# Issuing the K and V cache loads of an attention decode kernel from GpSimd instead of SyncE

## The chip, the cores and the metric

The kernel runs on one core of one Trainium2 chip. The metric is the device time of one execution in microseconds (us). A core has five engines that run their own instruction streams and meet at semaphores: TensorE (PE; its weight loads are shown apart as PEld), VectorE (DVE), ScalarE (ACT), GpSimd (POOL) and SyncE (SP). Sixteen DMA engines move data between the chip's memory (HBM) and the on-chip buffer of 128 partitions. A DMA is *issued* by an instruction in the stream of SP, ACT or POOL; the sixteen engines then work through its packets. SP's and ACT's DMAs have hardware descriptors, POOL's have descriptors that GpSimd's own software writes.

## What is computed

One new token goes through a gated mix of two blocks: attention over a long cache, and a small gated feed-forward network. With 32 heads, 65,536 cached positions and a head width of 128, the two caches hold 1,073.7 MB in bf16, and every byte is read once. The rest is small.

```python
q = (x @ wq).reshape(B, Sq, H, Dh)                       # 1 x 512 by 512 x 4096
scores = einsum("bhqd,bhkd->bhqk", q, k_cache) * Dh**-0.5  # H=32, Sk=65536, Dh=128
p = softmax(scores, axis=-1)
o = einsum("bhqk,bhkd->bhqd", p, v_cache)
a = o.reshape(B, Sq, H * Dh) @ wo                        # 4096 x 512
b = (silu(x @ w_gate) * (x @ w_up)) @ w_down             # 512 x 1792
g = sigmoid((x * gate_w).sum(-1))
return g * a + (1 - g) * b
```

## The kernel before

**Storage and halves.** One tile, `mem`, takes all loads. K and V of a head are each cut into two halves, z = 0 and z = 1. A half is 128 partitions of 256 positions of 128 bf16 values, so 65,536 bytes a partition in one run, 8.39 MB in all. There is one buffer for each of the four kinds of half, and they overlap in part: K's halves lie at `KA` and `KZ`, V's at `VA` and `VZ`. A load into a buffer can only start when what it overwrites has been read.

**The work on one head.** VectorE transposes K in sixteen chunks, eight for each half (`L329` for head 0, `L397` for z = 0 and `L404` for z = 1 of the others), into the double buffer `kt`. TensorE turns each chunk into scores (`L454`, 32 matmuls). `ktdone` counts transposed chunks, `qkdone` scored ones. When all scores of a head stand in `psS`, VectorE takes their maximum by partition (`L343`, counted by `s_mx`), GpSimd takes the maximum over the partitions (`L273`, `s_ar`), ScalarE scales it (`L298`), takes the exponentials with their sums (`L300`, `expdone`) and fetches the next head's query (`L303`, counted by `s_qc`), and GpSimd adds the sums over the partitions (`L275`, `s_L`). VectorE then shuffles the probabilities in two lots of 16 small copies (`L338`), one in the middle of the next head's first half of K and one after it. TensorE multiplies with V (`L501`, `pvdone`) one head later than the scores: V's half z of head h-1 is used right after the scores of half z of head h. Its 64 matmuls for each half stand in two parts, 40 and then 24, and each part raises `pvdone` by one, from a start value of 4.

**Loads.** SP issues nearly all of them, in one queue and in a fixed order. First come four weights (`L203`: wq, w_gate, w_up, w_down), then head 0's first K half in two pieces (`L217`), and then the loop's loads, all through one helper whose issue is `L213`. The order within the loop for head h is K z=0 of head h, V z=0 of head h-1, K z=1 of head h, V z=1 of head h-1. In front of each stands a wait for the work that frees its buffer:

```python
sp.wait_ge(ktdone, 2 * NP * h - 3 if h > 1 else NP);  load("k", h, 0)
sp.wait_ge(pvdone, 4 * h - 1);                        load("v", h - 1, 0)   # h > 1
sp.wait_ge(ktdone, 2 * NP * h + NP // 2);             load("k", h, 1)
sp.wait_ge(pvdone, 4 * h + 1);                        load("v", h - 1, 1)
```

Here `NP` is 8. After the loop come `wo` (`L235`), the last head's V in eight pieces (`L242`) and two rows of `wo` (`L244`, `L245`). ACT issues the loads of x and of the gate's weights, and the store of the output.

**GpSimd before.** It makes a few constant tiles at the start (`L249` to `L269`, among them the masks at `L255`), and then does nothing but its two sums over the partitions for each of the 32 heads. Ahead of the first mask and ahead of the first sum stands an instruction that makes a different set of GpSimd's routines ready (`MODIFY_POOL_CONFIG` in the trace).

Of the kernel before, what the change touches and what calls it, by code (L numbers as in the profile page):

```python
# [5 lines left out]
P = 128  # L6
KB = 512
PR = 32
NG = PR // 4

ALU = mybir.AluOpType
ACT = mybir.ActivationFunctionType
# [8 lines left out]
def bass_gated_mix__mha_block_cached__swiglu_ffn__decode_kernel(  # L21
# [11 lines left out]
    out: bass.AP,  # L33
):
    _, H, S, Dh = A_k_cache.shape
    D = A_wq.shape[0]
    F = B_w_gate.shape[1]
# [3 lines left out]
    HR = R // 2  # L41
    NP = HR // PR
# [5 lines left out]
    KA, KZ, VA, VZ, V0 = 32, 0, 120, 96, 96  # L48
# [10 lines left out]
    tail = [(32, 0, 128), (0, 128, 128), (V0 + 24, 256, 128), (V0 + 64, 384, 64),  # L59
            (V0 + 80, 448, 32), (V0 + 56, 480, 16), (V0 + 60, 496, 12), (V0 + 63, 508, 4)]  # L60
    WOJ, WO31 = V0, V0 + 1

    with ExitStack() as ctx:
# [6 lines left out]
        def sem(name):  # L70
            return ctx.enter_context(nc.semaphore(name))
# [35 lines left out]
        def at(kb, n):  # L107
            return mem[:, kb * KB:kb * KB + n]
# [9 lines left out]
        d = {n: sem("d_" + n) for n in names}  # L118
        dt_ = [sem(f"d_t{i}") for i in range(len(tail))]
# [16 lines left out]
        s_q = sem("s_q")  # L136
# [7 lines left out]
        s_b = sem("s_b")  # L144
        s_dch = sem("s_dch")
        ktdone = sem("ktdone")
        qkdone = sem("qkdone")
        pvdone = sem("pvdone")
# [26 lines left out]
        w_dram = {  # L175
            "wq": A_wq.rearrange("(p c) n -> p (c n)", c=Dc),
            "wg": B_w_gate.rearrange("(p c) f -> p (c f)", c=Dc),
            "wu": B_w_up.rearrange("(p c) f -> p (c f)", c=Dc),
            "wd": B_w_down.rearrange("(p c) n -> p (c n)", c=FC),
            "wo": A_wo.rearrange("(p j) n -> p (j n)", p=P),  # L180
        }
        wj_dram = w_dram["wo"][:, 31 * D:32 * D]
        w31_dram = A_wo.rearrange("(h d) n -> h d n", d=Dh)[H - 1]
        WQ, WG, WU, WD, WO = V0, 0, 14, V0 + 64, 64
# [5 lines left out]
        w2_ap = at(WOJ, 2 * D).rearrange("p (e c n) -> p e c n", e=2, c=4)  # L190
        ktb = [kt[:, b, :].bitcast(BF16).rearrange("p (j r m e) -> p j r m e", j=2, r=NG, e=2) for b in range(2)]

        def place(kind, h, z):
            if kind == "k":
                return (KA, V0)[z] if h == 0 else (KA, KZ)[z]
            return (VA, VZ)[z]

        def kv_dram(cache, h):
            return cache[0, h].rearrange("(b p r) d -> b p (r d)", b=2, p=P)

        for n, kb in (("wq", WQ), ("wg", WG), ("wu", WU), ("wd", WD)):
            src = w_dram[n]
# [3 lines left out]
        ctx.callback(lambda: nc.scalar.wait_ge(s_out, 16))  # L206
        block = ctx.enter_context(nc.Block())

        @block.sync
        def _(sp):  # L210
            def load(kind, h, z):
                cache = A_k_cache if kind == "k" else A_v_cache
                sp.dma_start(at(place(kind, h, z), HR * Dh), kv_dram(cache, h)[z]).then_inc(d[kind + "az"[z]], 16)  # L213

            half = HR // 2 * Dh
            for n in range(2):
                sp.dma_start(at(KA + 32 * n, half), kv_dram(A_k_cache, 0)[0][:, n * half:n * half + half]).then_inc(  # L217
                    (d["ka0"], d["ka"])[n], 16)
            sp.wait_ge(s_q, 1)
            load("k", 0, 1)  # L220
            for h in range(1, H):
                sp.wait_ge(ktdone, 2 * NP * h - 3 if h > 1 else NP)
                load("k", h, 0)
                if h == 1:
                    sp.wait_ge(ktdone, 2 * NP - 3)
                    sp.wait_ge(s_b, 1)
                else:
                    sp.wait_ge(pvdone, 4 * h - 1)
                load("v", h - 1, 0)
                sp.wait_ge(ktdone, 2 * NP * h + NP // 2)  # L230
                load("k", h, 1)
                sp.wait_ge(pvdone, 4 * h + 1)
                load("v", h - 1, 1)
            sp.wait_ge(ktdone, 2 * NP * H - NP)
            sp.dma_start(at(WO, 31 * D), w_dram["wo"][:, 0:31 * D]).then_inc(d["wo"], 16)  # L235
            src = A_v_cache[0, H - 1].rearrange("(b p r) d -> b p (r d)", b=2, p=P)
            need = {0: (ktdone, 2 * NP * H - 3), 1: (ktdone, 2 * NP * H), 2: (pvdone, 4 * H - 1)}
            for n, (kb, r0, nr) in enumerate(tail):
                if n in need:
                    sp.wait_ge(*need[n])  # L240
                b, o = divmod(r0, HR)
                sp.dma_start(at(kb, nr * Dh), src[b][:, o * Dh:(o + nr) * Dh]).then_inc(dt_[n], 16)  # L242
            sp.wait_ge(pvdone, 4 * H)
            sp.dma_start(at(WOJ, D), wj_dram).then_inc(d["wj"], 16)  # L244
            sp.dma_start(at(WO31, D), w31_dram).then_inc(d["w31"], 16)  # L245

        @block.gpsimd
        def _(pool):
            nc.gpsimd.memset(onesf[0:1, :], 1.0)  # L249
            nc.gpsimd.memset(sel, 0.0).then_inc(s_sel0, 1)  # L250
            pool.wait_ge(s_sel0, 1)
            for je in range(4):
                off = 64 * (je // 2) + je % 2
                v = sel[:, je, :].rearrange("p (g d) -> p g d", g=4)
                last = nc.gpsimd.affine_select(out=v, in_=v, compare_op=ALU.not_equal, fill=1.0, base=-off,  # L255
                                               pattern=[[0, 4], [-2, 32]], channel_multiplier=1)
            last.then_inc(s_sel, 1)
            nc.gpsimd.memset(unit[:], 0.0).then_inc(s_unit0, 1)
            pool.wait_ge(s_unit0, 1)
            nc.gpsimd.affine_select(out=unit[:], in_=unit[:], compare_op=ALU.not_equal, fill=1.0, base=0,  # L260
                                    pattern=[[-1, 4]], channel_multiplier=1).then_inc(s_unit, 1)
            nc.gpsimd.memset(bmat[:], 0.0).then_inc(s_b0, 1)
            for q in range(4):
                pool.wait_ge(s_b0, q + 1)
                nc.gpsimd.affine_select(out=bmat[:], in_=bmat[:], compare_op=ALU.not_equal, fill=1.0, base=-32 * q,
                                        pattern=[[-1, 32]], channel_multiplier=1).then_inc(s_b0, 1)
            nc.gpsimd.memset(hot[0:1, :, :], 0.0).then_inc(s_hot0, 1)
            pool.wait_ge(s_hot0, 1)
            nc.gpsimd.affine_select(out=hot[0:1, :, :], in_=hot[0:1, :, :], compare_op=ALU.not_equal, fill=1.0,  # L269
                                    base=0, pattern=[[1, 4], [-1, 4]], channel_multiplier=0).then_inc(s_hot, 1)  # L270
            for h in range(H):
                pool.wait_ge(s_mx, h + 1)
                nc.gpsimd.partition_all_reduce(amx, mxs, P, RMAX).then_inc(s_ar, 1)  # L273
                pool.wait_ge(expdone, h + 1)
                nc.gpsimd.partition_all_reduce(Lt, rsum, P, RADD).then_inc(s_L, 1)  # L275

        @block.scalar
        def _(act):
# [148 lines left out]
        def _(pe):  # L427
# [22 lines left out]
            def scores(z, c, u):  # L450
                col = 256 * z + PR * u
                for r in range(NG):
                    for je in range(4):
# [129 lines left out]
```

## Time and profile before

| What | Value |
|---|---|
| Median of 3 runs | 2520.21 us (2520.2 to 2520.8) |
| Span of the profiled execution | 2518.7 us |
| PE / PEld busy | 1584.6 / 890.1 us |
| DVE busy | 1397.8 us |
| ACT / POOL busy | 65.6 / 27.0 us |
| Read from HBM | 1087.77 MB, 432 GB/s over the span |

The profiled execution is one execution of the program. Its span runs from its first to its last instruction; the median of the timed runs is 1.5 us longer, which is the work around the span. The page gives busy time by engine, and then the span in 40 equal slices: for each the busy share of an engine in tenths, the mean busy share of the 16 DMA engines, and what they moved. Groups of instructions carry their line in the kernel, their number, their mean time and what ended the idle time ahead of them. "SPq" rows are SP's own DMA-issuing instructions; the time of such a row is that of the issue and not of the transfer. "POOLq" means the same for GpSimd.

### The profile page before, as it was taken

To read this page: it belongs to the slowest core of one execution; us is meant where nothing else is said; L and a number is where in the kernel's file an instruction comes from. 1 tells how busy PE (TensorE), PEld (TensorE's weight loads), DVE (VectorE), ACT (ScalarE), POOL (GpSimd) and SP (SyncE) were. 2 spreads that over 40 slices of the span, in tenths; PEclk is the share of its full clock that TensorE was granted. 3 is DMA by queue.
4 is the path that set the end of the run, shared out by engine and by line. 5 is a ranking of instruction groups with operands and counts; after the bars stand their busy time and mean duration, and the time that the engine had idled before them with its cause. 6 is when DMAs were issued, how large, how long until landed. Compare 5 with 4: busy or idle time off the path is not lost.

```text
span 2518.7 us, 46364 instructions
## 1 busy us (share of the span) xinstructions
PE 1584.6 (63%) x21432; PEld 890.1 (35%) x21432; DVE 1397.8 (55%) x1630; ACT 65.6 (3%) x195; POOL 27.0 (1%) x83
## 2 busy tenths in 40 slices
PE   3556756657666566565675665766656656567567
PEld 3333333333333333333333333333333333333334
DVE  3764565554654645646446555466464564644653
ACT  0000000000000000000000000000000000000000
POOL 0000000000000000000000000000000000000000
PEclk8567767677676776676776767767767767677676
DMA  9999999999999999999999999999999999999999
GB/s 421 432 433 434 434 434 433 433 433 433 433 433 433 433 433 434 433 436 433 433 434 432 433 434 433 433 433 434 433 433 433 437 434 433 433 433 434 433 433 390
DMA packets 20477, 1088.00 MB, mean 432 GB/s; under 512 B 2283, under 2 KB 2669, under 8 KB 2925
## 3 DMA queue, kind: packets, MB, share of 16 engines
q1 hardware_dynamic: 20448, 1087.78, 99.9%
q8 instruction: 11, 0.18, 0.0%
q14 instruction: 6, 0.04, 0.0%
q10 hardware_dynamic: 12, 0.00, 0.0%
HBM read 1087.77 MB, written 0.00 MB: 432 GB/s over the span
## 4 chain that ended last, share of the span: by engine, by line
DMA 73%; DVE 14%; issue 11%; PE 1%; DVEq 0%; SPq 0%; ACT 0%
DMA mem<-in_A_k_cache_dram 71%; DVE kt L404 7%; DVE kt L397 6%; DMA mem<-in_A_wo_dram 1%; PE psO L501 1%; DMA mem<-in_A_v_cache_dram 1%; DVE kt L329 0%; DVE pb L338 0%; DVEq L402 0%; SPq L203 0%; DVEq L395 0%; PE psZ L552 0%; PE psS L454 0%; SPq L217 0%; ACT fin L307 0%
## 5 line engine op out<-in xcount | busy, mean ns | idle before, releaser
L454 PE MATMUL psS<-qcur,kt 128*128 128x4 bf16 x16384 | 516.9, 166 | 887.0 <-DVE kt L397 552.5
L501 PE MATMUL psO<-mem,pb 128*4 128x512 bf16 x3968 | 999.8, 417 | 17.1 <-DMA mem<-in_A_v_cache_dram 17.1
L397 DVE STREAM_TRANSPOSE kt<-mem 128x2048 uint32<-128x2048 uint32 x248 | 551.2, 2280 | 578.5 <-DMA mem<-in_A_k_cache_dram 577.4
L454 PEld LDWEIGHTS psS<-qcur,kt 128*128 128x128 bf16 x16384 | 474.3, 104 | 955.7 <-DVE kt L397 585.7
L404 DVE STREAM_TRANSPOSE kt<-mem 128x2048 uint32<-128x2048 uint32 x248 | 547.6, 2275 | 407.5 <-DMA mem<-in_A_k_cache_dram 407.5
L501 PEld LDWEIGHTS psO<-mem,pb 128*4 128x4 bf16 x3968 | 354.3, 91 | 619.1 <-issue 186.2
L338 DVE COPY pb<-pa 32x64 bf16<-32x64 bf16 x1024 | 233.7, 228 | 25.9 <-PE psO L501 11.1
L329 DVE STREAM_TRANSPOSE kt<-mem 128x2048 uint32<-128x2048 uint32 x16 | 35.4, 2279 | 16.9 <-DMA mem<-in_A_k_cache_dram 16.9
L343 DVE TENSOR_REDUCE sm<-psS 128x1 f32<-128x512 f32 x32 | 22.1, 692 | 35.5 <-PE psS L454 35.5
L294 ACT ACTIVATE oTn<-psT,gcol 128x1 bf16<-128x1 f32 x31 | 8.2, 263 | 1111.6 <-PE psT L481 1111.6
L273 POOL PARTITION_ALL_REDUCE sm<-sm x32 | 11.3, 352 | 2391.2 <-DVE sm L343 2391.2
L481 PEld LDWEIGHTS psT<-unit,orow 4*128 4x128 f32 x256 | 30.8, 186 | 14.9 <-issue 13.5
L481 PE MATMUL psT<-unit,orow 4*128 4x1 f32 x256 | 33.5, 248 | 0.8 <-ACT orow L292 0.8
L292 ACT ACTIVATE orow<-psO,sm 4x512 f32<-4x512 f32 x31 | 21.0, 678 | 446.8 <-issue 446.8
L298 ACT ACTIVATE sm<-sm 128x1 f32<-128x1 f32 x32 | 6.5, 203 | 832.1 <-POOL sm L273 832.1
L300 ACT ACTIVATE pa<-psS,sm 128x512 bf16<-128x512 f32 x32 | 22.0, 687 | 1.0
L515 PE MATMUL psW<-pb,mem 128*128 128x1 bf16 x512 | 14.3, 165 | 7.1 <-DMA mem<-in_A_v_cache_dram 6.0
L515 PEld LDWEIGHTS psW<-pb,mem 128*128 128x128 bf16 x512 | 13.9, 102 | 8.1 <-issue 6.4
L275 POOL PARTITION_ALL_REDUCE sm<-sm x32 | 12.3, 385 | 36.4 <-ACT pa L300 36.4
L438 PE MATMUL psM<-xTb,mem 128*128 128x1 bf16 x128 | 3.6, 165 | 11.5 <-DMA mem<-in_A_wq_dram 11.5
L424 DVE TENSOR_SCALAR w<-psW,sm 128x4 bf16<-128x4 f32 x1 | 0.2, 226 | 17.5 <-PE psW L515 17.5
L466 PE MATMUL psM<-xTb,mem 128*128 128x1 bf16 x112 | 6.9, 198 | 4.6 <-DMA mem<-in_B_w_up_dram 4.6
(63 smaller groups left out, 64.1 us busy)
## 6 DMA issues: line engine op xcount, KB each, us to landing
mem<-in_A_v_cache_dram SPq DMA_DIRECT2D x3, 4096.0 KB, 27.8
mem<-in_A_k_cache_dram SPq DMA_DIRECT2D x2, 4096.0 KB, 38.9
mem<-in_A_wq_dram SPq DMA_DIRECT2D x1, 4096.0 KB, 13.0
mem<-in_A_wo_dram SPq DMA_DIRECT2D x1, 3968.0 KB, 33.8
mem<-in_A_v_cache_dram SPq DMA_DIRECT2D x1, 2048.0 KB, 32.3
mem<-in_B_w_gate_dram SPq DMA_DIRECT2D x1, 1792.0 KB, 16.9
mem<-in_B_w_up_dram SPq DMA_DIRECT2D x1, 1792.0 KB, 21.4
mem<-in_B_w_down_dram SPq DMA_DIRECT2D x1, 1792.0 KB, 25.2
```

Of the source, the lines that this page charges most:

```text
L275: nc.gpsimd.partition_all_reduce(Lt, rsum, P, RADD).then_inc(s_L, 1)
L292: nc.scalar.mul(orow[0:4, :], psO[0:4, :], Li[0:4, :]).then_inc(s_or, 1)
L300: nc.scalar.activation(pa[:], psS[:], ACT.Exp, bias=nbias, scale=SCALE, accum_out=rsum).then_inc(expdone, 1)
L329: nc.vector.transpose(kt[:, i % 2, :].rearrange("p (j r t) -> p r j t", j=2, t=32), src.rearrange("p (r j t) -> p r j t", j=2, t=32)).then ...
L338: last = nc.vector.tensor_copy(dst, sr)
L343: nc.vector.reduce_max(mxs, psS[:], AX_X).then_inc(s_mx, 1)
L397: nc.vector.transpose(kt[:, c % 2, :].rearrange("p (j r t) -> p r j t", j=2, t=32), src.rearrange("p (r j t) -> p r j t", j=2, t=32)).then ...
L404: nc.vector.transpose(kt[:, c % 2, :].rearrange("p (j r t) -> p r j t", j=2, t=32), src.rearrange("p (r j t) -> p r j t", j=2, t=32)).then ...
L454: last = nc.tensor.matmul(psS[:, col + 4 * r:col + 4 * r + 4], ktb[c % 2][:, je // 2, r, :, je % 2], qcur[:, je, :], start=(je == 0), stop ...
L481: last = nc.tensor.matmul(psT[:, 0:1], orow[0:4, i * Dh:(i + 1) * Dh], unit[0:4, i:i + 1], start=(i == 0), stop=(i == 3))
L501: last = nc.tensor.matmul(psO[0:4, :], pb[:, 256 * z + r:256 * z + r + 4], vt[:, r * Dh:(r + 4) * Dh], start=(z == 0 and part == 0 and m = ...
L515: last = nc.tensor.matmul(psW[:, 0:1], vt[:, r * Dh:(r + 1) * Dh], pb[:, col:col + 1], start=(col == 0), stop=(col == R - 1))
```

## The change

The loop of loads moves from SP's stream into GpSimd's, with the same order and the same waits. SP keeps the four weights at the start. Four things differ besides the issuing engine:

- The two pieces of head 0's first K half wait for w_up to have landed (`d["wu"]`); before, they followed the weights in SP's queue with no wait.
- GpSimd's two sums for head h-1 (`peaks`) now stand in the same stream as the loads: for h > 1 behind the issue of K z=0 of head h and ahead of V z=0 of head h-1; for h = 1 behind V z=0 of head 0; for the last head ahead of the third piece of the tail.
- The instruction that makes the sums' routines ready now stands where the first sum stands, behind the issue of V z=0 of head 0.
- Each moved DMA carries the argument `single_packet=False`.

```diff
+ONE = False
...
-        @block.sync
-        def _(sp):
...
+        def load(eng, kind, h, z):
+            cache = A_k_cache if kind == "k" else A_v_cache
+            eng.dma_start(at(place(kind, h, z), HR * Dh), kv_dram(cache, h)[z],
+                          single_packet=ONE).then_inc(d[kind + "az"[z]], 16)
...
-            for h in range(H):
+            def peaks(h):
                 pool.wait_ge(s_mx, h + 1)
                 nc.gpsimd.partition_all_reduce(amx, mxs, P, RMAX).then_inc(s_ar, 1)
                 pool.wait_ge(expdone, h + 1)
                 nc.gpsimd.partition_all_reduce(Lt, rsum, P, RADD).then_inc(s_L, 1)
+
+            half = HR // 2 * Dh
+            pool.wait_ge(d["wu"], 16)
+            for n in range(2):
+                pool.dma_start(at(KA + 32 * n, half), kv_dram(A_k_cache, 0)[0][:, n * half:n * half + half],
+                               single_packet=ONE).then_inc((d["ka0"], d["ka"])[n], 16)
+            pool.wait_ge(s_q, 1)
+            load(pool, "k", 0, 1)
+            for h in range(1, H):
+                pool.wait_ge(ktdone, 2 * NP * h - 3 if h > 1 else NP)
+                load(pool, "k", h, 0)
+                if h == 1:
+                    pool.wait_ge(ktdone, 2 * NP - 3)
+                    pool.wait_ge(s_b, 1)
+                    load(pool, "v", 0, 0)
+                    peaks(0)
+                else:
+                    peaks(h - 1)
+                    pool.wait_ge(pvdone, 4 * h - 1)
+                    load(pool, "v", h - 1, 0)
+                pool.wait_ge(ktdone, 2 * NP * h + NP // 2)
+                load(pool, "k", h, 1)
+                pool.wait_ge(pvdone, 4 * h + 1)
+                load(pool, "v", h - 1, 1)
...
+            for n, (kb, r0, nr) in enumerate(tail):
+                if n in need:
+                    pool.wait_ge(*need[n])
+                if n == 2:
+                    peaks(H - 1)
+                b, o = divmod(r0, HR)
+                pool.dma_start(at(kb, nr * Dh), src[b][:, o * Dh:(o + nr) * Dh], single_packet=ONE).then_inc(dt_[n], 16)
```

More of the change, by code (lines that the diff above doesn't have):

```diff
@@ L207, in bass_gated_mix__mha_block_cached__swiglu_ffn__decode_kernel @@
         block = ctx.enter_context(nc.Block())
-        @block.sync
-        def _(sp):
[L211 to L245, printed above, removed]
+        def load(eng, kind, h, z):
+            cache = A_k_cache if kind == "k" else A_v_cache
+            eng.dma_start(at(place(kind, h, z), HR * Dh), kv_dram(cache, h)[z],
+                          single_packet=ONE).then_inc(d[kind + "az"[z]], 16)
         @block.gpsimd
@@ L275, in _ @@
                 nc.gpsimd.partition_all_reduce(Lt, rsum, P, RADD).then_inc(s_L, 1)
+            half = HR // 2 * Dh
[21 more added lines that the diff above has]
+                load(pool, "v", h - 1, 1)
+            pool.wait_ge(ktdone, 2 * NP * H - NP)
+            pool.dma_start(at(WO, 31 * D), w_dram["wo"][:, 0:31 * D], single_packet=ONE).then_inc(d["wo"], 16)
+            src = A_v_cache[0, H - 1].rearrange("(b p r) d -> b p (r d)", b=2, p=P)
+            need = {0: (ktdone, 2 * NP * H - 3), 1: (ktdone, 2 * NP * H), 2: (pvdone, 4 * H - 1)}
+            for n, (kb, r0, nr) in enumerate(tail):
[5 more added lines that the diff above has]
+                pool.dma_start(at(kb, nr * Dh), src[b][:, o * Dh:(o + nr) * Dh], single_packet=ONE).then_inc(dt_[n], 16)
+            pool.wait_ge(pvdone, 4 * H)
+            pool.dma_start(at(WOJ, D), wj_dram, single_packet=ONE).then_inc(d["wj"], 16)
+            pool.dma_start(at(WO31, D), w31_dram, single_packet=ONE).then_inc(d["w31"], 16)
         @block.scalar
```

## The prediction

> **What bounds the kernel now.** I read the page's slices and DMA queues first, because 1,088 MB in 2,519 us suggests the transfers.
>
> ```profile
> DMA  9999999999999999999999999999999999999999
> GB/s 421 432 433 434 434 434 433 433 433 433 433 433 433 433 433 434 433 436 433 433 434 432 433 434 433 433 433 434 433 433 433 437 434 433 433 433 434 433 433 390
> ...
> q1 hardware_dynamic: 20448, 1087.78, 99.9%
> ```
>
> SP's queue (q1) keeps all sixteen DMA engines in work for 99.9% of the span, at a flat 433 GB/s. Only the first and last slices are lower. No compute engine is above 63%. So time can change in two ways only: a packet takes another time, or an engine of the sixteen runs dry.
>
> What does a packet take? Of the trace's packet records, 16,000 are of 65,536 bytes (one partition's run of one half of K or V), with a median of 2,422 ns and 90% of them within 2,418 to 2,426. Smaller ones of the same queue: 32,768 bytes 1,213 ns, 16,384 bytes 611, 8,192 bytes 309, 4,096 bytes 159. Sixteen of the last for one of the first is 2,544 against 2,422, so a packet costs about (2,544 - 2,422) / 15 = 8 ns beside its bytes. Laid end to end by engine, the records leave 1 us idle per engine from the start of the loads to their end.
>
> Next, how near the queue comes to running dry: SP's timeline, for five loads of steady running, and then the last line of the answer on the loads' own line, L213.
>
> ```profile
> 119.62 0.33 SPq L213 DMA_DIRECT2D mem<-in_A_v_cache_dram  x1
> 135.50 0.33 SPq L213 DMA_DIRECT2D mem<-in_A_k_cache_dram  x1
> 154.39 0.33 SPq L213 DMA_DIRECT2D mem<-in_A_v_cache_dram  x1
> 172.00 0.33 SPq L213 DMA_DIRECT2D mem<-in_A_k_cache_dram  x1
> 195.88 0.33 SPq L213 DMA_DIRECT2D mem<-in_A_v_cache_dram  x1
> ```
>
> ```profile
> DMA to landing us min/median/max: 23.7/27.5/48.6
> ```
>
> A half takes 8.39 MB / 433 GB/s = 19.4 us on the wire. The shortest issue to landing is 23.7 us, so even that load stood 4.3 us between issue, queue and completion. By the packet records, and by kind of load, the wait from issue to the first packet is about 8 us for K z=1, 6 for K z=0, 5.5 to 7 for V z=0, and for V z=1 only 1.8 to 3.8 us on the engine that is first free and 3.9 to 5.4 on the last one. On an empty queue the first weight's packets start 1.0 us after its issue. So V z=1 has some 1 to 3 us to spare on the first engine and 3 to 4 on the last, and the others 4 or more.
>
> **The change part by part.**
>
> *125 issues of halves move from SP to POOL.* An SP issue row is 0.33 us. No row shows a software descriptor. The nearest rows of POOL are its memset of 0.52 us and its sum of 0.35; the farthest is the 12.6 us gap below. I take 1 us more than SP to the first packet, near the short rows. The cover of the tightest load is 1 us on the first engine and about 3 on the last, and a half lands with its last engine, so the price is 0. Where the cover is gone, each us beyond it costs 31 us, because V z=1 comes 31 times.
>
> *Bytes and packets.* The same 128 runs of 65,536 bytes move. I take the packet at 2,422 ns, so 0. The bounds: cut into 4,096-byte packets, 125 halves x 8 packets an engine x 122 ns = +122 us; all eight runs of an engine joined in one packet, 125 x 7 x 8 ns = -7 us.
>
> *The sums stand between the loads.* For h > 1 POOL waits for `s_mx` ahead of V z=0, and nothing but that load and those behind it are queued there. The rows of head 1:
>
> ```profile
> 143.94 0.35 POOL L273 PARTITION_ALL_REDUCE sm<-sm  x1 [56.32 <-DVE sm L343]
> 145.43 0.39 POOL L275 PARTITION_ALL_REDUCE sm<-sm  x1 [1.14 <-ACT pa L300]
> ```
>
> The second sum ends at 145.8, and the load behind it was issued at 154.39, since its own wait (`pvdone`, 40 matmuls of V) comes later. Cover 8.6 us, cost 0. In the other direction, the load ahead of the sums (K z=0, 135.50) has 8.4 us before 143.94 to be issued in. In the tail the sums end at 2468.5 and the third piece waits for 40 matmuls that begin at 2466.36 and take 10.45, so until 2476.8; the eight pieces and two rows have some 30 us in the queue, so ten issues of 1 us cost 0.
>
> *The start.* The two pieces of head 0's first half were queued at 2.70 us; now they wait for w_up, which TensorE sees at 23.1. Behind w_up there is only w_down, 1.835 MB or 4.2 us. The first engine is through with it at 24.9, the last at about 26.5. Issued at 23.2 with 1 to 2 us to the first packet, the cost is 0 to 0.5 us; I take 0.2. The next two loads' waits (`s_q` at 17.4, `ktdone` at 55.7) are as before.
>
> *The routines for the sums.* They are made ready once; before, GpSimd's idle time hid it. The trace shows what this took ahead of the first mask:
>
> ```profile
> 0.86 0.52 POOL L250 MEMSET mem<- 128x512 bf16 x1
> 13.98 1.11 POOL L255 TENSOR_SCALAR_AFFINE_SELECT mem<-mem 128x128 bf16<-128x128 bf16 x4 [12.60 <-issue]
> ...
> 85.70 0.38 POOL L273 PARTITION_ALL_REDUCE sm<-sm  x1 [68.32 <-DVE sm L343]
> ```
>
> Before, the second such step began at 17.6 us and had until 85.7. Now it begins behind the issue of V z=0 of head 0, at 77.2 + 1 us. At 12.6 us it ends at 90.8, so head 0's maximum is 5.1 us late. ScalarE's exponentials and the next head's query (`qcur`) are as late; TensorE cannot score head 1's first chunk, and VectorE stops ahead of its third (90.2 in the trace of before) for about 3.5 us. K z=1 of head 1 moves from 94.6 to 98.1 and has 7.7 us; V z=1 of head 0 moves from 119.62 to 123.1, with a first packet 2 us later at 125.1, against engines free at 121.8 to 123.8. That is 1.3 us dry on the last engine. Once, and never made up, since the queue has no other gaps: +1.3. From nothing (if it takes under 7.5 us) to +3.
>
> *Sum.* 2520.2 + 0.2 + 1.3 = 2521.7 us, or 2520.2 on the span of 2518.7.
>
> **Rules weighed.** The Trainium skill, page "DMA: Bandwidth & Descriptors", section "Measured (HBM→SBUF, 128 partitions, SWDGE, issued from GpSimd)", gives 425 GB/s for its largest software-descriptor transfer; no run here shows it, and by it the sum would be about 2520 x 433 / 425 = 2567 us, an estimate from that page. The same page's table of latencies says that two of the sixteen engines are usually slower, perhaps because the descriptor rings share their ports; the trace of before, with hardware descriptors, has no such engine (90% of packets within 8 ns).
>
> **The rivals.**
>
> *Dry queue (slower).* The path from POOL's wait to the first packet is longer than V z=1's cover. It decides from about 4.4 us (the middle of 3.9 to 5.4). At 6 us it costs 31 x 1.6 = +50, so 2570; at 5 us, 2540. For it: no row shows that path, and GpSimd's only longer step took 12.6 us. Against it: its ordinary steps take 0.1 to 0.5 us, and POOL answered VectorE's maximum in 0.14 us (from 85.56 to 85.70).
>
> *Dearer packets (slower).* Runs cut finer, or some engines slower. Cut to 16,384 bytes: 4 x 611 - 2,422 = 22 ns, x 1,000 packets an engine = +22, so 2543; to 4,096: 2642; engines that take 1% longer: 2545. For it: 65,536 is the largest packet that the trace shows, and nothing says that software writes that size. Against it: bytes and rows are the same. The page's 425 belongs to this rival.
>
> *Cheaper packets (faster).* GpSimd joins an engine's runs: 2521.7 - 7 = 2514 to 2515. Against it: 8 of 2,422 ns is all there is to win, and packets here never held more than one run.
>
> *VectorE holds GpSimd up (slower).* K z=1 is issued where the copies begin:
>
> ```profile
> 171.90 3.85 DVE L338 COPY pb<-pa 32x64 bf16<-32x64 bf16 x16
> 175.78 8.89 DVE L397 STREAM_TRANSPOSE kt<-mem 128x2048 uint32<-128x2048 uint32 x4
> ```
>
> If POOL could write no descriptor until the copies end, 3.9 us of 8.2 are gone and nothing is lost. If the four transposes held it too, 12.7 us would pass against 9.8 on the last engine: +4 us with the path, 31 times, 2645. The Trainium skill, page "SBUF — State Buffer", section "SBUF: two separate sides", says that some of VectorE's two-port operations lock GpSimd out of writing descriptors until they end; no run here shows it.
>
> **How the numbers follow.** A measurement of this kernel can tell about 0.2%, or 5 us, from no change. Covers hold, 2515 to 2525: 0.46. Cheaper packets: 0.12. Dearer packets: 0.21. Dry queue: 0.13. VectorE's hold: 0.04. Routines that take over 17 us to be made ready, one loss of 6 to 20 us: 0.04. So faster 0.12, same 0.46, slower 0.42. The range goes from 2513 (cheaper packets with none of the one-time costs, 2520.2 - 7) up to 2575, which takes in the dry queue at 6 us, 16,384-byte packets and engines up to 2% slower; finer cuts and the hold stay out. The likeliest case's own range is 2517 to 2525.
>
> **What would show it.** In the changed profile: the large queue is now POOL's, still at 99 to 100% and 433 GB/s, with as many packets; its issue to landing for V z=1 stays between 23 and 26 us; L273's counterpart has a first wait that ends near 91 and not 85.7; K's and V's waits by VectorE and TensorE stay as long as they were. A DMA share below 99% in all slices would mean the dry queue or the hold; a share of 100% at fewer GB/s would mean dearer packets; more GB/s, cheaper ones. Forecast 2521.7 us.

## The result, and the profile after

| Kernel | Median of the runs (us) | Lowest to highest | Ratio to before, 95% interval |
|---|---|---|---|
| before, 9 runs | 2520.2 | 2519.75 to 2520.8 | 1 |
| after, 9 runs | 2526.88 | 2523.22 to 2532.85 | 1.0027 [1.0019, 1.0036] |

The changed kernel is 0.27% slower. It lies inside the range of 2513 to 2575. It stands 5 us above the forecast of 2521.7, and 2 us above the upper end of the likeliest case (2525); four of its nine runs are inside that case. The spread is new as well: before, nine runs lay within 1 us, and now they lie within 10. The profiled execution is one of the four shorter ones: 2524.83 us with a span of 2523.4, so its span is 4.7 us longer than before's 2518.7. What follows is about these 4.7 us first.

The page's slices and queues of the changed kernel:

```profile
GB/s 414 424 432 432 432 431 432 433 433 431 432 432 436 435 433 433 434 432 432 436 432 433 432 432 432 432 434 432 433 433 432 434 437 436 432 434 432 432 431 386
...
q0 software_dynamic: 19520, 1078.08, 98.9%
q1 hardware_dynamic: 576, 9.70, 0.9%
```

The two queues together are at 99.8%, where SP's alone was at 99.9%. The first two slices fell from 421 and 432 GB/s to 414 and 424; many of the others read 432 where 433 stood. Nothing collapsed: a little is lost at the start, and a little everywhere. The queues have 352 packets fewer than before (20,448). They are runs of the tail's last pieces: 384 packets of 1,024 bytes and 128 of 3,072 have become 96 of 4,096 and 64 of 6,144. So the software descriptors joined the smallest runs, and left the 16,000 of 65,536 bytes as they were.

GpSimd's timeline, the start and the first loads of the loop (the last bracket is the idle time ahead and what ended it):

```profile
23.13 1.41 POOL L248 DMA_DIRECT2D mem<-in_A_k_cache_dram  x2 [6.50 <-DMA mem<-in_B_w_up_dram]
24.54 0.53 POOL L212 DMA_DIRECT2D mem<-in_A_k_cache_dram  x1
57.34 0.53 POOL L212 DMA_DIRECT2D mem<-in_A_k_cache_dram  x1 [32.28 <-DVE kt L335]
...
89.96 0.38 POOL L241 PARTITION_ALL_REDUCE sm<-sm  x1 [10.29 <-issue]
...
97.47 0.74 POOL L212 DMA_DIRECT2D mem<-in_A_k_cache_dram  x1 [5.59 <-DVE kt L403]
122.48 0.54 POOL L212 DMA_DIRECT2D mem<-in_A_v_cache_dram  x1 [24.28 <-PE psO L507]
```

The issue of a load takes GpSimd 0.53 to 0.74 us. The first sum ends its wait at 89.96 (before 85.70), and V z=1 of head 0 is issued at 122.48 (before 119.62). K z=0 of head 1 is issued at 57.34; before, that was 55.66.

How long GpSimd takes to answer is seen in the chain of waits. Here is the same place in both kernels, before first: VectorE's last transposes, "issue" (nothing the profile shows was waited for), and the load.

```profile
365.40 2.28 DVE kt L404
367.68 0.02 issue
367.69 27.48 DMA mem<-in_A_k_cache_dram
```

```profile
367.65 2.28 DVE kt L410
369.94 0.28 issue
370.22 28.19 DMA mem<-in_A_k_cache_dram
```

SP answered in 0.02 us, GpSimd in 0.28. Behind that stands the step from issue to first packet on an engine with nothing to do. In the packet records it is, at the shortest, 1.0 us with hardware descriptors and 1.25 us with software ones. So the shortest path is some 0.5 us longer. It is not always that short: of the changed kernel's 22 first packets of V z=1 that stand behind a gap, half came 2.5 us or more after the issue.

Last, the answer on the loads' line (L212):

```profile
DMA to landing us min/median/max: 22.3/27.2/43.2
```

The shortest transfer takes 22.3 us where it took 23.7. A shorter stay in the queue is no gain here: the load came later, against engines that were nearly free.

**Packet records, both kernels.** These are the 16,000 packets of 65,536 bytes of each profiled execution. "Long" are those over 2,440 ns; "excess" is what they took over 2,422 ns, and "idle" are the gaps between packets, without those of a few ns, both per engine of the sixteen. The records do not name the engine; packets are put in line by their times.

| | Median (ns) | Long | Longest (ns) | Excess (us) | Idle (us) | Last packet ends (us) |
|---|---|---|---|---|---|---|
| before | 2,422 | 26 | 3,045 | 0.5 | 0.7 | 2515.9 |
| after | 2,420 | 284 | 4,053 | 4.0 | 2.2 | 2520.6 |

Excess and idle grew by 3.5 and 1.5 us, the end of the data by 4.7. The long packets are not spread evenly. The packets that begin within 7.5 us of an issue of V z=1 hold 2.9 us of the excess and 1.0 us of the idle time; the start holds most of the other idle time; no other kind of load holds more than 0.5 of the excess. A 65,536-byte packet that follows a gap of over 300 ns takes a median of some 2,950 ns (about 20 packets), and not 2,420.

So an engine that runs dry pays twice: the gap, and then some 0.5 us for the packet after it.

How near did the loads come to that? Call *cover* the time from a load's issue until an engine is through with the load ahead of it. From the issue of V z=1, the previous load was over on the first engine after 2.95 us and on the last after 4.69 in the median before. In the changed kernel these are 2.75 and 4.31 us. Each load raises its semaphore sixteen times, once for each engine, and these landings, some 0.5 us behind the packets' ends, show the same: the spread over the engines is 1.7 us before and 1.6 us after. So the engines do not drift apart, and the loss is the sum of what each of them loses at each issue.

The lowest cover matters. In the changed kernel the first engine was free less than 2.5 us after the issue in 14 of the 31 loads of V z=1, and these hold 3.6 of V z=1's 3.9 us of excess and idle time. Before, 8 loads were as near and lost 0.3 us in all. The lowest values were 1.9 us before, and 0.1 (head 0) and 0.8 us after.

### The profile page after: what moved, and what is told of

Same layout as the page of the kernel before. It is cut to its first block, busy times and chain, and to the rows that moved or that the text cites. A ratio compares the mean times of both kernels' runs of the same rounds, so it can differ in the third digit from the quotient of the medians.

```text
span 2523.4 us, 46365 instructions
## 1 busy us (share of the span) xinstructions
PE 1587.7 (63%) x21432; PEld 890.0 (35%) x21432; DVE 1398.5 (55%) x1630; ACT 65.7 (3%) x195; POOL 101.8 (4%) x221
## 3 DMA queue, kind: packets, MB, share of 16 engines
q0 software_dynamic: 19520, 1078.08, 98.9%
## 4 chain that ended last, share of the span: by engine, by line
DMA 72%; DVE 14%; issue 12%; PE 1%; POOL 0%; DVEq 0%; ACT 0%; SPq 0%
DMA mem<-in_A_k_cache_dram 69%; DVE kt L410 7%; DVE kt L403 6%; DMA mem<-in_A_v_cache_dram 2%; PE psO L507 1%; DMA mem<-in_B_w_up_dram 1%; DVE kt L335 1%; DVE pb L344 0%; PE psS L460 0%; DVEq L408 0%; POOL mem L278 0%; POOL mem L248 0%; DVEq L401 0%; PE psZ L558 0%; SPq L204 0%
## 5 line engine op out<-in xcount | busy, mean ns | idle before, releaser
L212 POOL DMA_DIRECT2D mem<-in_A_v_cache_dram x62 | 34.1, 550 | 1043.9 <-PE psO L507 996.8
L212 POOL DMA_DIRECT2D mem<-in_A_k_cache_dram x63 | 33.6, 533 | 1013.0 <-DVE kt L403 510.8
L444 PE MATMUL psM<-xTb,mem 128*128 128x1 bf16 x128 | 3.6, 165 | 11.3 <-DMA mem<-in_A_wq_dram 11.3
(70 smaller groups left out, 80.4 us busy)
```

What stands on the lines that cost most here:

```text
L212: eng.dma_start(at(place(kind, h, z), HR * Dh), kv_dram(cache, h)[z], single_packet=ONE).then_inc(d[kind + "az"[z]], 16)
```

## Experiments

The theory after this reading: *the tightest load (V z=1) reaches engines that are just free, and the start is late; what the software does to the packets themselves is nearly nothing*. The rivals: that software descriptors cost time of their own on every load (dearer packets), or that the sums and issues standing in one stream on GpSimd are what delays them. All times are medians, and ratios are against runs of the kernel before on the same chip (2519.98 to 2520.06).

| Run | us | Lowest to highest | Ratio, 95% interval |
|---|---|---|---|
| V z=1 on SP | 2526.22 | 2524.62 to 2527.1 | 1.0024 [1.0014, 1.0034] |
| V z=0 on SP | 2611.94 | 2610.13 to 2612.88 | 1.0365 [1.0351, 1.0379] |
| head 0's K on SP, routines early | 2527.07 | 2525.36 to 2538.64 | 1.0028 [1.0017, 1.0038] |
| V z=1 cut in two | 2524.99 | 2524.28 to 2526.55 | 1.0021 [1.0011, 1.003] |
| before, V z=1 cut in two | 2522.45 | 2522.25 to 2522.77 | 1.0009 [1.0001, 1.0018] |
| start early | 2523.14 | 2520.57 to 2535.33 | 1.0024 [1.0013, 1.0036] |
| start early and V z=1 cut | 2523.04 | 2522.78 to 2523.38 | 1.0011 [1.0002, 1.002] |
| before, V z=1 later by 4 matmuls | 2539.46 | 2536.73 to 2544.68 | 1.0081 [1.0068, 1.0094] |
| before, V z=1 later by 1 matmul | 2538.28 | 2536.03 to 2540.51 | 1.0075 [1.0058, 1.0092] |
| after, V z=1 later by 4 matmuls | 2554.74 | 2550.45 to 2557.13 | 1.0132 [1.0115, 1.0149] |
| single_packet on | 2528.49 | 2527.77 to 2532.33 | 1.0034 [1.002, 1.0048] |
| before, V z=0 issued by ACT | 2611.1 | 2608.8 to 2615.2 | 1.0365 [1.0348, 1.0382] |

### Back to SP, one kind of load at a time

V z=1 alone returns to SP and its hardware descriptors:

```diff
-                pool.wait_ge(pvdone, 4 * h + 1)
-                load(pool, "v", h - 1, 1)
...
+        @block.sync
+        def _(sp):
+            for h in range(1, H):
+                sp.wait_ge(pvdone, 4 * h + 1)
+                load(sp, "v", h - 1, 1)
```

> The changed kernel with only V z=1's 31 loads handed back to SP (hardware descriptors); the other loads stay with GpSimd. Theory 'dry queue': what the change costs after the start comes from V z=1, whose first packets come later than the leading DMA engines run out of work. Then the growth after the first 130 us goes, and the start's 1.7 us (head 0's K waits for w_up) and at most 1.6 us (sums' routines) stay: 2521.5 to 2523.5 us, the spread of the 65,536-byte loads over the engines back from 5 us to about 2. Rival 'every software load costs something': 94 of 125 loads still are software's, so some three quarters of +6.7 stay: about 2525 us.

It came out at 2526.22, near the changed kernel, and so by its time nearer to the rival's 2525 than to the theory's range. But the excess in long packets fell from 4.0 to 1.7 us per engine, and the last V z=1 was issued at 2442.59, against 2446.55 in the changed kernel and 2441.51 before. So up to there nearly all was won back. The time went in the tail. The chain's end shows the last V z=1 (first number: start, second: issue to landing):

```profile
2432.31 10.26 PE psO L511 x40
...
2442.59 33.64 DMA mem<-in_A_v_cache_dram
```

It landed 33.64 us after its issue, where before it took 24.80. GpSimd no longer waited with V z=1, so it had issued `wo` at 2431.53, 11 us ahead of V z=1 and no longer behind it, and the two queues were served side by side. The run had therefore not changed one thing only, and its time decides nothing on its own.

The second such run puts V z=0 on SP in place of V z=1, with the same edit around the wait on `4 * h - 1`:

```diff
-                    pool.wait_ge(pvdone, 4 * h - 1)
-                    load(pool, "v", h - 1, 0)
...
+                    sp.wait_ge(pvdone, 4 * h - 1)
+                load(sp, "v", h - 1, 0)
```

> The changed kernel with only V z=0's 31 loads handed back to SP; V z=1 stays with GpSimd. 'Dry queue': V z=0 had 5 to 7 us in the queue, so nothing is won: 2524 to 2530 us, as the changed kernel, with long first packets at V z=1 as there. Rival 'every software load costs something': as much won as with V z=1, about 2525 us, and V z=1's packets no worse than others'.

2611.94 us: over 91 us slower than before, which nothing had led me to expect. Its chain runs through loads of K z=0 that landed late, here for two heads. The first line is the same kind of load in the kernel before:

```profile
1219.20 27.49 DMA mem<-in_A_k_cache_dram
```

```profile
1181.88 32.47 DMA mem<-in_A_k_cache_dram
...
1261.59 32.25 DMA mem<-in_A_k_cache_dram
```

To see whether this came from software beside hardware or from two queues at all, the kernel *before* was run with V z=0 issued by ACT, so with hardware descriptors throughout:

```diff
-                else:
-                    sp.wait_ge(pvdone, 4 * h - 1)
-                load("v", h - 1, 0)
...
+                    if h > 0:
+                        act.wait_ge(pvdone, 4 * h + 3)
+                        act.dma_start(at(VA, HR * Dh), kv_dram(A_v_cache, h)[0]).then_inc(d["va"], 16)
```

> The kernel before with V z=0's loads issued by ACT (ahead of its row scaling) and all others by SP: both are hardware descriptors, but two queues. It tells why e2 took 2612 us. If two queues share the engines packet by packet, so that V z=0 takes half of the rate from K z=0 which is needed first: K lands late, the chain from K to the next issue is late, and the time is near e2's: 2590 to 2620 us. If e2's loss came from mixing software and hardware descriptors: 2520 to 2523 us.

2611.1 us, the same loss, and no software descriptor in it. Its page (queues, with share of the sixteen engines' span) and its chain in the same place:

```profile
q1 hardware_dynamic: 15984, 827.73, 74.3%
q10 hardware_dynamic: 4476, 260.05, 23.1%
```

```profile
1180.08 32.20 DMA mem<-in_A_k_cache_dram
...
1260.45 34.51 DMA mem<-in_A_k_cache_dram
```

K's first halves are issued every 80.4 us (1260.45 - 1180.08); in the kernel before, two of the chain's loads of K one head apart begin at 1178.30 and 1255.71, 77.4 us apart. Three us for each of 31 heads are the 91 us. The queues add up to 97.4% where one queue had 99.9%, which is some 65 us of this span, and long packets hold 25 us per engine; together these are the 91 us too. Software is not the cause.

The landings show the sharing. In the run with ACT, the V z=1 ahead had landed at 1188.08, so from there K z=0 needed 19.4 us, until 1207.5, had it been alone. It landed at 1212.28, 4.8 us later, and V z=0 had been issued at 1199.27 from the other queue and was served beside it. In the run with SP it is 4.8 us too (1214.34 against 1209.6). I read the rest as the loss of order: in one queue, V z=0 waits behind K; in two, it takes packets from a K half that is needed sooner, and the engines later stand idle for a buffer that is not yet free (in the ten us from 1240 to 1250 the DMA share is 0.78, where before it was 1.00). In the run with ACT its row scaling also stands behind V z=0's wait; in the run with SP it does not, and the loss is the same. So putting a part back on SP does not simply undo the change.

### The start

Head 0's K goes back to SP, and a sum over a constant column makes GpSimd's routines ready early:

```diff
+            for n in range(2):
+                sp.dma_start(at(KA + 32 * n, half), kv_dram(A_k_cache, 0)[0][:, n * half:n * half + half]).then_inc(
+                    (d["ka0"], d["ka1"])[n], 16)
+            sp.wait_ge(s_q, 1)
+            sp.dma_start(at(V0, HR * Dh), kv_dram(A_k_cache, 0)[1]).then_inc(d["kz1"], 16)
...
+            nc.gpsimd.memset(sm[:, 7:8], 0.0).then_inc(s_first, 1)
+            pool.wait_ge(s_first, 1)
+            nc.gpsimd.partition_all_reduce(sm[:, 8:9], sm[:, 7:8], P, RMAX)
```

> The changed kernel with the start undone: head 0's three K loads are issued by SP as before the change, and a first sum over the partitions, on an unused column, makes the routines ready at some 17 to 30 us. All other loads stay with GpSimd. If the start costs 1.7 + 1.6 us, as the profiled execution has it, this is 3.3 us faster than the changed kernel: about 2523.5 us, and K z=0 of head 1 is issued at 55.7 and V z=1 of head 0 at 119.6 again. 'Dry queue': the long first packets at V z=1 stay, and so some 3 us and a spread over runs. Rival 'all of the cost is at the start': 2520 to 2521 us.

2527.07, no gain, where 2523.5 was expected. VectorE's timeline (of the slowest run, 2538.64) says why: K z=1 of head 0 now shared the wire with K z=0 of head 1, from the other queue.

```profile
73.16 17.66 DVE L342 STREAM_TRANSPOSE kt<-mem 128x2048 uint32<-128x2048 uint32 x8 [17.73 <-DMA mem<-in_A_k_cache_dram]
```

These transposes began at 66.10 in the kernel before. The start had become later by 7 us instead of earlier, so this run does not show what the late start costs.

The start was tried again with one queue for the cache: GpSimd waits for the weight wq instead of w_up, and the routines are made ready early as above.

```diff
-            pool.wait_ge(d["wu"], 16)
+            pool.wait_ge(d["wq"], 16)
```

> The changed kernel with a cleaner start inside GpSimd's own queue: head 0's K loads wait for wq (13.4 us) and not for w_up (23.1), so they stand in the queue well before w_down ends, and a first sum on an unused column right behind them makes the routines ready at some 18 to 30 us. No load goes back to SP, so no two queues share the engines later. If the start costs 1.7 + 1.6 us: K z=0 of head 1 issued at 55.7, V z=1 of head 0 at 119.6, and the data end 1.7 to 3.3 us sooner than in the changed kernel, if V z=1's losses stay as large: 2521.5 to 2525 us. 'Dry queue' adds: the losses at V z=1 do not go, since that cover is as before; the long first packets stay there.

2523.14, and the spread from 2520.57 to 2535.33 over 12 runs is wider than ever; a few of them draw up the ratio. GpSimd's timeline:

```profile
16.64 1.41 POOL L249 DMA_DIRECT2D mem<-in_A_k_cache_dram  x2 [0.32 <-issue]
...
85.72 0.35 POOL L242 PARTITION_ALL_REDUCE sm<-sm  x1 [7.65 <-DVE sm L353]
...
119.40 0.53 POOL L213 DMA_DIRECT2D mem<-in_A_v_cache_dram  x1 [24.04 <-PE psO L511]
```

The first sum is back at 85.72 and V z=1 of head 0 at 119.40, both as before the change. That took the one-time losses away, and the best run stands 0.6 us from the kernel before. V z=1's losses stay: 2.0 us of excess per engine in the profiled run, in some heads and not in others.

### Cover for V z=1

The rows 0 to 95 of V z=1's buffer are free earlier than the rest. Here V z=1 is loaded in two pieces, and the first is issued right behind K z=1:

```diff
+                pool.wait_ge(pvdone, 4 * h)
+                part(pool, h - 1, 0, V_KEEP)
                 pool.wait_ge(pvdone, 4 * h + 1)
-                load(pool, "v", h - 1, 1)
+                part(pool, h - 1, V_KEEP, HR)
...
-                        pe.wait_ge(d["v" + "az"[z]], i * 16)
+                        pe.wait_ge(d["v" + "az"[z]], i * (16, 32)[z])
```

> The changed kernel with V z=1's load cut in two: rows 0 to 95, which lie in no other buffer, are issued by GpSimd right behind K z=1, some 20 us earlier; rows 96 to 255 at the old place. The queue then holds 7 us more when the second is issued. It adds 31 x 8 packets an engine, at 8 ns 2 us. 'Dry queue': the long packets and idle time at V z=1 go, the start's 1.7 to 3.3 us stay: 2522 to 2525.5 us, the runs within 1 us of each other. Rival 'every software load costs something': one load more a head, so slower than the changed kernel: over 2527 us.

The cut itself costs something: one more packet for each row. Its price is that of the same edit in the kernel before:

> The kernel before, all loads on SP, with V z=1's load cut in two as in e4 (rows 0 to 95 right behind K z=1). Nothing ran dry there, so only the cut's own price is left: 31 x 8 more packets an engine at 8 ns, 2 us: 2521 to 2523 us. If cutting costs nothing, 2520.2, and then all of e4's +4.8 belongs to the start and to software descriptors.

2522.45 there, 2.4 us over the kernel before: 31 x 8 more packets on each engine at 8 ns are 2.0. In the changed kernel the cut gave 2524.99. Net of its price that is 2522.6, against 2526.88 without it, and the runs lie within 2.3 us and no longer within 10 (1 us was expected). In the timeline the first piece follows K z=1 at once:

```profile
98.34 0.74 POOL L212 DMA_DIRECT2D mem<-in_A_k_cache_dram  x1 [5.59 <-DVE kt L408]
99.09 0.53 POOL L216 DMA_DIRECT2D mem<-in_A_v_cache_dram  x1
123.08 0.53 POOL L216 DMA_DIRECT2D mem<-in_A_v_cache_dram  x1 [23.45 <-PE psO L512]
```

The excess in long packets fell from 4.0 us to 0.7 per engine, and of the 7,936 packets of V z=1's two pieces a single one is long.

Both together, the early start (with its early routines) and the cut:

> Both remedies with all loads in GpSimd's queue: e11's start and e4's early piece of V z=1. 'Dry queue' plus the start account for everything: the time of e10, 2521 to 2523 us, within 1 us of it, with under 1 us of long packets and idle. Rival 'software descriptors cost something beside the start and V z=1': 2 us or more over e10.

2523.04, within 0.6 us over 11 runs. That is 0.6 us above the same cut with hardware descriptors. The page:

```profile
GB/s 421 425 441 433 433 433 430 437 433 434 434 424 439 436 433 433 433 428 438 433 433 433 433 432 433 433 433 432 432 438 433 433 434 428 439 433 433 434 429 391
...
q0 software_dynamic: 23984, 1078.08, 99.0%
```

The steady slices are back at 433 and 434, the excess is 0.4 us per engine, and 99% of the 65,536-byte packets took 2,418 to 2,428 ns. All loads of the cache still have software descriptors, and the sums still stand between them. With cover they cost 0.6 us of 2,520, so neither rival holds.

The runs give the whole difference in terms, but how it divides hangs on the order. With the cover first, it is 2526.88 - (2524.99 - 2.4) = 4.3 us for V z=1's cover and 2524.99 - 2523.04 = 2.0 for the start and the routines. With the start first, it is 2526.88 - 2523.14 = 3.7 for the start and the routines and 2523.14 - (2523.04 - 2.4) = 2.5 for the cover. The rest is 0.6 both ways. All this holds so far as the cut costs GpSimd what it cost SP, and the two medians without the cut are of runs that spread over 10 and 15 us.

### Taking the cover away

If cover is the cause, the kernel before must lose time in the same way when V z=1 is issued later, with hardware descriptors. The issue waits for four of the matmuls of the second part too (2.1 us):

```diff
-                sp.wait_ge(pvdone, 4 * h + 1)
+                sp.wait_ge(s_late, h)
...
+                                if z == 0 and part == 1 and m == 3:
+                                    last.then_inc(s_late, 1)
```

> The kernel before, all loads on SP with hardware descriptors, but V z=1 is issued 2.1 us later: it waits for the fifth instead of the first point after 40 matmuls (one turn of 1.05 us and four matmuls of 0.26). 'Dry queue' as a matter of cover alone: 1.0 + 2.1 us to the first packet against 1.8 to 3.8 us on the leading engine, as in the changed kernel, so long first packets and idle time at V z=1 appear with hardware descriptors too: 2522 to 2530 us. Rival 'software's first packets are slow by themselves': within 1 us of 2520.2.

```profile
GB/s 418 430 430 429 430 430 431 431 427 419 427 430 432 441 433 430 429 418 441 430 427 433 431 430 430 430 429 431 430 430 435 427 428 429 432 429 430 430 437 393
...
q1 hardware_dynamic: 20448, 1087.78, 99.7%
```

2539.46, 19.5 us slower, far more than the 2522 to 2530 that was expected: 962 long packets, 15.7 us of excess and 6.8 us idle per engine. This is the changed kernel's picture, three to four times as strong, and there is no software in it. With one matmul more in place of four (`m == 0`, 1.3 us):

> The kernel before, all loads on SP, with V z=1 issued 1.3 us later (one turn and one matmul). It gives the point from which lateness costs, with hardware descriptors: 1.0 + 1.3 us to the first packet against 1.8 to 3.8 on the leading engine. 'Dry queue': about the lateness that software's path has in the changed kernel, so about its time, 2522 to 2530 us, well under e5's 2539.5. If 1.3 us costs nothing, software's path is longer by more than that.

2538.28. I had expected a fraction of that, and 1.3 us cost nearly as much as 2.1. The kernel before stood close to an edge. By the landings, the first engine was free within 1.9 us of the issue in 20 of this run's 31 loads of V z=1, which lost some 0.77 us each; with four matmuls it was 24 loads and 0.80 us each. Beyond the edge, the number of loads that are hit decides, and hardly how late they are. The changed kernel with the delay of four matmuls:

> The changed kernel with V z=1 issued by GpSimd 2.1 us later, by the same wait as in e5 (4 matmuls into the second part). 'Dry queue': software's path is some 1 to 2.5 us longer than hardware's, so now nearly all engines run dry each time: e5's +19.5 us and 31 times 1 to 2.5 more, 2550 to 2600 us. Rival 'V z=1's cost in the changed kernel is a fixed one per load': 2.1 us later changes it by little, under 2535 us.

```profile
q0 software_dynamic: 19520, 1078.08, 98.3%
```

2554.74, 28 us above the changed kernel, with 20.7 us of excess and 18.5 idle. The same delay costs more when the path is 0.5 us longer, as it should if both use up one cover.

### The packets

```diff
-ONE = False
+ONE = True
```

> The changed kernel with single_packet=True on all moved loads. The prediction's rival of cheaper packets: if an engine's eight runs become one packet, at 8 ns for each packet saved, 7 us off the wire time; the start and V z=1 stay: 2517 to 2521 us, with some 2,000 long packet records in place of 16,000. If the argument changes nothing on the wire: as the changed kernel, 2523 to 2533 us.

```profile
q0 software_dynamic: 19520, 1078.08, 98.8%
```

The same 19,520 packets in the queue, 16,000 of 65,536 bytes as without it: the argument joined nothing and gained nothing. 2528.49 lies within the runs of the changed kernel (2523.22 to 2532.85).

## Why the prediction was right and where it failed

**The number.** 2526.88 lies inside the range, but that is owed to the range's width, which was made for rivals that did not come true. The likeliest case, "covers hold", ended at 2525, and its forecast of 2521.7 had 1.5 of the 6.7 us. What happened is nearest to the dry queue, which had a chance of 0.13. Of the signs that were named, the queues' 99.8% and the first sum near 91 us came; V z=1's issue to landing, at 22.3 us at the shortest, fell out of its 23 to 26 and showed the lost cover.

**Right: the wire.** The kernel is still bound by transfers, and with cover the software queue carries 433 GB/s in packets of 2,420 to 2,422 ns. The large runs were neither cut nor joined, so the dearer and the cheaper packets both fall. (That a packet never holds more than one run did not stay so for the tail's smallest runs, and is worth some 0.2 us at 8 ns a packet.) The Trainium skill, page "DMA: Bandwidth & Descriptors", section "Measured (HBM→SBUF, 128 partitions, SWDGE, issued from GpSimd)", has 425 GB/s for its largest transfer, by which the sum was estimated at 2567. Here the measured 433 decides. Nor are some engines slower: in the run with start and cover 99% of the 65,536-byte packets are within 10 ns.

**Right: the sums, and the delay by the routines.** The first sum came at 89.96 (forecast 90.8) and V z=1 of head 0 at 122.48 (forecast 123.1). It found five engines idle for up to 1.7 us. The loss there is 0.7 us per engine, half of it in long packets, where 1.3 had been taken from the last engine alone. Between later loads the sums cost nothing: V z=0 is still released by V's matmuls.

**Right in its result, by a wrong order: the tail.** I had the last head's sums end at 2468.5, ahead of the third piece's wait. They stand behind that wait, as GpSimd's timeline shows:

```profile
2481.37 0.35 POOL L241 PARTITION_ALL_REDUCE sm<-sm  x1 [12.17 <-PE psO L507]
2482.85 0.39 POOL L243 PARTITION_ALL_REDUCE sm<-sm  x1 [1.14 <-ACT pa L306]
2483.11 3.22 POOL L278 DMA_DIRECT2D mem<-in_A_v_cache_dram  x6
```

The six pieces are issued about 1.7 us later for it. The queue's stock hid this: from 2372.1 to 2518.8 us no engine stood idle for over 0.2 us.

**Wrong: the start, 0.2 us.** K z=0 of head 1 was issued 1.7 us late. Start and routines together, forecast at 1.5 us, cost 2.0 by the runs with the cut and 3.7 by those without. The wait for w_up ended as forecast (23.13), but the first packets came 1.85 to 3.5 us behind it and not 1 to 2, so six engines stood idle for 0.9 to 1.8 us. The two pieces' issue alone takes 1.41 us.

**Wrong: V z=1, priced at 0.** This is the step that failed. The prediction had the first engine's cover (1.8 to 3.8 us to the first packet), set a path of 2 us against it, and then let the *last* engine decide, "a half lands with its last engine". The shortest path was shorter than assumed, and the price was still 2.5 to 4.3 us. A leading engine that runs dry does not wait for the last one at no cost. It loses its gap and a longer first packet, and the queue has no other gaps in which to make that up: the mean excess and idle time of an engine over the span, 5.0 us more than before, is about the 4.7 us by which the data end later. The spread of 10 us between runs goes with it: the early start with no cut, which has V z=1's losses left, varies as much, and the two runs with the cut do not.

**The dry-queue rival** named the mechanism, but its point and its price were both off. It was to begin at 4.4 us, the last engine's figure, and to cost 31 us for each us beyond. Losses began where the first engine was free some 2.5 us after the issue; and at 1.3 and 2.1 us more, the kernel before lost 18 and 19.5 us, so the price is no straight line.

**VectorE's hold** was not seen. K z=1's issue rows are 0.53 to 0.74 us, and from head 2 on that load took 29.3 to 29.5 us from issue to landing, where it had taken 29.7 to 30.0; a hold of 12.7 us against a cover of 8 to 9.8 would have made it longer. A hold by the copies alone (3.9 us) would be hidden and is left open. The Trainium skill, page "SBUF — State Buffer", section "SBUF: two separate sides", lets some of VectorE's operations lock GpSimd out of writing descriptors. No run here shows such a hold, and none rules it out for every operation; it costs nothing here.

**Left open.** Why engines have packets of 2,450 to 4,053 ns even where no gap stands ahead of them; why software's loads lose at a cover of 2 to 2.5 us when their shortest path is 1.25 (the hardware ones of the kernel before lose next to nothing there); what makes one run of the same program start such a run of losses and another not.

## What to carry to other kernels

In a kernel bound by one queue, read the cover of each load on the engine that is free first, and at its lowest, not at landing. A slower issuing path costs nothing only where that is longer than the path, and longer than the path's shortest value: here losses all but stopped at a cover of some 2.5 us, twice the 1.25. If it is not, issue a free part of the buffer early, as the cut of V z=1 does. Keep loads whose order matters in one queue, since a second one shares the wire and undoes the order.

## What was not expected of the hardware

- An engine that has run dry takes a median of some 2,950 ns (3,100 in the kernel before with V z=1 2.1 us late) for its next 65,536-byte packet, instead of 2,420.
- The shortest path of a load from GpSimd is only some 0.5 us longer than from SP: 0.28 us to answer instead of 0.02, and 1.25 us to the first packet instead of 1.0.
- Moving V z=0's loads to a second queue costs 91 us, with software beside hardware (2611.94) and with hardware alone (2611.1).
- The argument `single_packet` changed neither the number of packets nor their size. Software descriptors joined runs of 1,024 and 3,072 bytes into packets of 4,096 and 6,144 either way.
